# Splitting an MLP's tokens into two passes, with a seven-product scheme and DMA sums in the second

## The chip, the cores and the metric

The kernel runs on one core of one Trainium2 chip. The metric is device time in microseconds, from runs of the whole kernel; the profile beside it describes one further execution, by the hardware profiler. Five engines matter here: TensorE (PE; its weight loads are shown apart as PEld), VectorE (DVE), ScalarE (ACT), GpSimd (POOL) and SyncE (SP), which issues the DMAs. Each works through its own instructions in order; they wait for each other by semaphores.

## The reference, cut to what matters

```python
B, S, D, F, H = 1, 2048, 576, 4608, 32          # tokens, width, hidden width, heads

def reference(x, wqkv, wo, w1, w2, w3, w4):
    xn = layernorm(x)
    # A: each token attends to 8 earlier positions, 2 apart, 32 heads of 18
    q, k, v = heads(xn @ wqkv)
    a = softmax(q . k[pos - 0, 2, ..., 14] * 18 ** -0.5)      # masked where pos < 0
    A = (a . v[same positions]) @ wo
    # B: shifted mixing, then an MLP
    h  = gelu(layernorm(xn) @ w1)                # four channel quarters, shifted by +1 -1 +2 -2 tokens
    x1 = xn + shifted(h) @ w2
    B  = x1 + gelu(layernorm(x1) @ w3) @ w4      # w3: 576 x 4608, w4: 4608 x 576
    return x + A + B
```

All arrays are float32. The kernel multiplies in a reduced-precision form (`F32R`) and keeps accuracy by splitting each operand into a high and a low half: a product is high by high, high by low and low by high.

## The kernel before, in words

A multiplication on TensorE takes at most 128 rows of depth. The depth 576 is four blocks of 128 and a rest of 64; the rest's high and low halves lie together in one block of 128 rows. That gives the 14 pairs of `PAIRS`: one tile of depth 576 is 14 multiplications.

The stages, in order:

1. Projection: x is normalised, transposed and multiplied with wqkv; q, k and v go to DRAM.
2. Mixing (`mix_tile`, `mix_rem`, `w2_tile`): the shifted layer. `Y[:, t, :]`, 16 tiles of 128 tokens by 576, holds x1 afterwards. `n_turn` normalises and transposes the tiles, by way of DRAM (`put`, `get`, `split_x`), into four blocks `x1n[b]` of 512 tokens.
3. The MLP, a loop over 72 units `(c, b)` (L829): c is a block of 256 hidden channels (18), b a block of 512 tokens (4). `up(c, b, i)` (L742) makes one tile of 128 hidden channels by 512 tokens, 14 multiplications into PSUM; ACT takes the gelu twice, once rounded to the high half, once exact (L750, L751), and DVE subtracts to get the low half (L752). `down(c, b, j)` (L755) multiplies 128 tokens of the unit before with w4, 12 multiplications of 288 columns, and DVE adds the result from PSUM to `Y` in SBUF (L769). The weights of the next block are loaded by SP (`load_f`) and split by ACT and DVE (`split_w`, L167 and L168).
4. Attention itself runs on DVE during the MLP. `attention` is a generator of DVE operations, each with a price in us; `bg(us)` adds to a budget (capped at 1.5) and issues operations until it is spent. The unit calls it six times with 6.1 / 6. Eight groups of four heads; q, k and v come back from DRAM, the result goes to DRAM (`od`).
5. Output: the attention result is transposed like x1, multiplied with wo (28 multiplications of 288 columns per 128 tokens), added to `Y` on DVE and stored.

The order is written out by hand (`manual_schedule`): each engine gets its instructions in the order in which the program names them. PSUM has two tiles of 512 columns (`psa`, for up) and three of twice 512 (`psb`, for down). What a buffer of a pool holds must be read before the pool gives it out again; that, and not a plan, sets how far an engine may run ahead.

Of the kernel before, what the change touches and what calls it, by code (L numbers as in the profile page):

```python
# [19 lines left out]
HD = 18  # L20
# [25 lines left out]
def fused_block(ctx, tc, x, wqkv, wo, w1, w2, w3, w4, out):  # L46
# [7 lines left out]
    ring = ctx.enter_context(tc.tile_pool(name="ring", bufs=2, side="right", reuse_waits="tile"))  # L54
# [4 lines left out]
    Y = base.tile([128, NT, D], F32, name="Y")  # L59
# [6 lines left out]
    BN = base.tile([128, 4, 2, 6], F32, name="bn")  # L66
    ST = RT = None
# [31 lines left out]
    def transposes(src, tail, xt, col):  # L99
# [9 lines left out]
        act.copy(xt[:, 0:4, c], p0)  # L109
        for i in range(rows // 64):  # L110
            xtt, ct = tail[1][i]
            act.copy(xtt[0:64, 4, ct:ct + 128], p1[64 * i:64 * i + 64])
        dve.tensor_tensor(xt[:, 5:9, c], p0, xt[:, 0:4, c].bitcast(F32), op=ALU.subtract)  # L113
        for i in range(rows // 64):
            xtt, ct = tail[1][i]
            dve.tensor_tensor(xtt[64:128, 4, ct:ct + 128], p1[64 * i:64 * i + 64],
                              xtt[0:64, 4, ct:ct + 128].bitcast(F32), op=ALU.subtract)
# [21 lines left out]

    def get(key, xt):  # L140
        for k in ((0, 3), (3, 5)):
            sp.dma_start(xt[:, 4 + k[0]:4 + k[1], :].bitcast(F32),
                         xd[key][k[0]:k[1]].rearrange("k p c -> p k c"))

    def split_x(xt, part=None):
        raw = xt.bitcast(F32)
        if part != 1:
            act.copy(RT[64:128, :], raw[64:128, 4, :])
            act.copy(xt[0:64, 4, :], raw[0:64, 4, :])
            dve.tensor_tensor(xt[64:128, 4, :], raw[64:128, 4, :], RT[64:128, :].bitcast(F32),  # L150
                              op=ALU.subtract)
        for h in range(2) if part is None else (part,):
            hi, lo = slice(2 * h, 2 * h + 2), slice(2 * h + 5, 2 * h + 7)
            act.copy(xt[:, hi, :], raw[:, lo, :])
            dve.tensor_tensor(xt[:, lo, :], raw[:, lo, :], raw[:, hi, :], op=ALU.subtract)
# [35 lines left out]
    def z_turn(t):  # L191
        z = w1pool.tile([128, D], F32, name="z", bufs=1)
        norm(z, Y[:, t, :], 1, t)
# [14 lines left out]
    def norm_x(t):  # L208
        norm(Y[:, t, :], xtile[t], 0, t)
        if t >= 4:  # L210
            dve.tensor_copy(tail_half(t), Y[:, t, 512:])

    def ring_block(key):
        if key not in xring:
            xring[key] = ring.tile([128, 9, 512], F32R, name="xt", tag="xt")
        return xring[key]

    def prep_x(t):
        xt = ring_block(("q", t // 4))
        if t < 4:  # L220
            tail = (Y[:, t, 512:], [(xt, t * 128)])
        else:
            tail = pair_tail(ztail[t // 2], xt, t)
        transposes(Y[:, t, :], tail, xt, (t % 4) * 128)
# [33 lines left out]
    zpad = qpool.tile([16, HALO * GC], F32, name="zpad")  # L258
    pool.memset(zpad, 0.0)

    def lhs(t):
        xt = xring[("q", t // 4)]
        c = (t % 4) * 128
        return lambda s: xt[:, s, c:c + 128]
# [41 lines left out]
    def x_prep(t):  # L306
        prep_x(t)
        stats(Y[:, t, :], 1, t)

    def x_turn(t):  # L310
        stats(xtile[t], 0, t)
        norm(Y[:, t, :], xtile[t], 0, t)
        turn(Y[:, t, :], t % 4)
        stats(Y[:, t, :], 1, t)
# [30 lines left out]
    sp.dma_start(dram_ap(qkvd[8:9, 0:1, :], 0, [[(HALO + S) * GC, 16], [1, HALO * GC]]), zpad)  # L345
# [35 lines left out]
    for cg in range(1, 5):  # L381
        for t in range(4):
# [5 lines left out]
            if cg == 1:  # L388
                stats(Y[:, t, :], 1, t)
# [3 lines left out]
    def q_last(b):  # L393
        rawp.__exit__(None, None, None)
        xring["q", b] = lastp.__enter__().tile([128, 9, 512], F32R, name="xl")
# [55 lines left out]
    def load_w2(k):  # L451
        if k == 2:
            r = mupool.tile([128, D], F32, name="rz2", bufs=1)
# [13 lines left out]
    def mix_tile(b, m):  # L467
        xt = xring[("z", b)]
        ps = psa.tile([128, 512], F32, name="p1", tag="a")
        for i, (a, w) in enumerate(PAIRS):  # L470
            pe.matmul(ps, W1[:, w, m * 128:(m + 1) * 128], xt[:, a, :],  # L471
# [10 lines left out]
    def mix_rem(b):  # L482
        xt = xring[("z", b)]
        ps = psa.tile([128, 512], F32, name="p1", tag="a")
        for a in range(9):
            pe.matmul(ps, W1R[:, a if a < 5 else a - 5, :], xt[:, a, :], start=a == 0, stop=a == 8)  # L486
        u = mupool.tile([128, 512], F32, name="u", bufs=2)
        v = mupool.tile([128, 512], F32, name="v", bufs=2)
# [24 lines left out]
    def n_turn(t, zpool):  # L513
        z = zpool.tile([128, D], F32, name="rz", tag="rz")
        act.activation(z, Y[:, t, :], AF.Identity, bias=RS[2][:, t, 0:1], scale=RS[2][:, t, 1:2])
# [4 lines left out]
    def w2_tile(t):  # L520
# [10 lines left out]
        yv = Y[:, t, :].rearrange("p (h c) -> p h c", h=2)  # L531
# [423 lines left out]
```

## Time and profile before

| what | value |
|---|---|
| median of 3 runs | 1293.11 us (1292.91 to 1293.54) |
| the profiled execution's own time | 1293.05 us |
| its span, first to last instruction | 1291.3 us |
| PE busy | 1282.4 us, 99% |
| DVE busy | 939.2 us, 73% |
| ACT busy | 363.1 us, 28% |
| POOL busy | 36.7 us, 3% |
| moved by DMA | 130.45 MB, mean 101 GB/s |
| MLP stage (first up to last down) | about 313 to 1229 us |

"Busy" is the share of the span in which an engine had an instruction in hand. The rows of a profile name a line, an engine, an operation, what it writes and reads, how often it came, its busy time, the mean time of one in ns, and the idle time before it with what ended that.

### The profile page before, as it was taken

How to read it: one execution, taken by the hardware profiler on the slowest of the kernel's cores; microseconds unless marked ns; L12 is line 12 of the kernel's file. 1: busy time of each engine (PE TensorE's matmuls, PEld its weight loads, DVE VectorE, ACT ScalarE, POOL GpSimd, SP SyncE). 2: the span in 40 equal slices, each digit the busy share in tenths (PEclk: the TensorE clock that was granted, in tenths of full speed). 3: DMA queues.
4: the chain of work that ended last, by engine and by line, in shares of the span. 5: the costliest groups of instructions: out<-in, count | busy, mean ns of one | idle time of the engine just before them, and what ended most of it. 6: DMA issues, size and time to landing. Idle time of an engine off the chain costs nothing.

```text
span 1291.3 us, 18505 instructions
## 1 busy us (share of the span) xinstructions
PE 1282.4 (99%) x7642; PEld 1181.3 (91%) x7642; DVE 939.2 (73%) x1334; ACT 363.1 (28%) x593; POOL 36.7 (3%) x108
## 2 busy tenths in 40 slices
PE   8999999999999999999999999999999999999999
PEld 8999998999999998989999999999898999999998
DVE  6775424778676778888878888878888978855841
ACT  3332225444422232231222132232232231212410
POOL 2110000111000000000000000000000000000000
PEclk9999999999999999999999999999999999999999
DMA  7698994247602130221221221220222011156742
GB/s 213 180 199 172 209 195 118 69 106 195 198 29 72 31 100 20 81 82 39 82 72 49 82 73 45 85 72 30 80 94 72 30 48 46 56 121 155 211 145 83
DMA packets 165189, 130.45 MB, mean 101 GB/s; under 512 B 73569, under 2 KB 135905, under 8 KB 165105
## 3 DMA queue, kind: packets, MB, share of 16 engines
q1 hardware_dynamic: 165104, 129.27, 37.1%
q8 instruction: 60, 0.98, 0.3%
q14 instruction: 25, 0.20, 0.0%
HBM read 86.18 MB, written 42.01 MB: 99 GB/s over the span
## 4 chain that ended last, share of the span: by engine, by line
PE 97%; DVE 1%; DMA 1%; ACT 0%; issue 0%; SPq 0%; POOL 0%; ACTq 0%; DVEq 0%
PE ps L766 35%; PE p L746 35%; PE ps L182 19%; PE p L471 3%; PE ps L286 2%; PE p L486 0%; DMA raw<-in_A_wqkv_dram 0%; DVE bn L86 0%; PE p L923 0%; DVE WQ L168 0%; DMA qkvd<-stg 0%; DMA xin<-in_A_x_dram 0%; PE ps L104 0%; DVE xt L113 0%; DVE Y L96 0%
## 5 line engine op out<-in xcount | busy, mean ns | idle before, releaser
L766 PE MATMUL ps<-W,hi 128*128 128x288 f32 x2304 | 398.6, 294 | 0.0
L766 PEld LDWEIGHTS ps<-W,hi 128*128 128x128 f32 x2304 | 339.4, 188 | 6.5 <-DVE Y L769 0.2
L750 ACT ACTIVATE hi<-p 128x512 fp32r<-128x512 f32 x144 | 86.2, 599 | 582.2 <-PE p L746 582.2
L766 PE MATMUL ps<-W,lo 128*128 128x288 f32 x1152 | 245.3, 294 | 0.0
L746 PE MATMUL p<-x1n,W 128*128 128x512 f32 x1008 | 234.6, 389 | 0.0
L746 PE MATMUL p<-xt,W 128*128 128x512 f32 x1008 | 234.5, 389 | 0.0
L746 PEld LDWEIGHTS p<-xt,W 128*128 128x128 f32 x1008 | 187.3, 188 | 36.9
L746 PEld LDWEIGHTS p<-x1n,W 128*128 128x128 f32 x1008 | 187.3, 188 | 36.9
L769 DVE TENSOR_TENSOR Y<-ps,Y 128x576 f32<-128x576 f32 x288 | 211.8, 748 | 10.9 <-PE ps L766 10.7
L752 DVE TENSOR_TENSOR lo<-g,hi 128x512 fp32r<-128x512 f32 x144 | 99.4, 690 | 159.9 <-ACT g L751 159.7
L766 PEld LDWEIGHTS ps<-W,lo 128*128 128x128 f32 x1152 | 185.3, 187 | 0.0
L182 PE MATMUL ps<-WQ,xt 128*128 128x432 f32 x448 | 88.4, 359 | 0.0
L182 PEld LDWEIGHTS ps<-WQ,xt 128*128 128x128 f32 x448 | 84.3, 188 | 3.9
L698 DVE TENSOR_TENSOR prod<-q,k 128x1152 f32<-128x1152 f32 x64 | 86.3, 1349 | 0.0
L701 DVE TENSOR_REDUCE L<-prod 128x64 f32<-128x1152 f32 x64 | 86.1, 1345 | 0.0
L751 ACT ACTIVATE g<-p 128x512 f32<-128x512 f32 x144 | 85.4, 593 | 0.0
L682 DVE TENSOR_TENSOR o<-o,prod 128x1152 f32<-128x1152 f32 x56 | 75.5, 1348 | 0.0
L678 DVE TENSOR_TENSOR prod<-v,L 128x1152 f32<-128x1152 f32 x56 | 75.5, 1348 | 0.0
L167 ACT CAST W<-rawf 128x640 fp32r<-128x640 f32 x72 | 50.3, 700 | 70.3 <-PE ps L766 69.2
L168 DVE TENSOR_TENSOR W<-rawf,W 128x640 fp32r<-128x640 f32 x72 | 56.1, 782 | 0.0
L182 PE MATMUL ps<-W,h 128*128 128x288 f32 x384 | 53.4, 295 | 0.0
L471 PE MATMUL p<-xt,W 128*128 128x512 f32 x224 | 52.9, 391 | 0.3 <-ACT g L477 0.3
(117 smaller groups left out, 967.7 us busy)
## 6 DMA issues: line engine op xcount, KB each, us to landing
xd<-st SPq DMA_DIRECT2D x56, 320.0 KB, 6.0
rawf<-in_B_w_dram SPq DMA_DIRECT2D x36, 288.0 KB, 3.1
rawf<-in_B_w_dram SPq DMA_DIRECT2D x36, 256.0 KB, 3.0
xt<-xd SPq DMA_DIRECT2D x9, 768.0 KB, 6.3
qkvd<-stg SPq DMA_DIRECT2D x64, 108.0 KB, 3.8
xin<-in_A_x_dram SPq DMA_DIRECT2D x16, 288.0 KB, 3.8
xt<-xd SPq DMA_DIRECT2D x9, 512.0 KB, 7.2
q<-qkvd SPq DMA_DIRECT2D x8, 576.0 KB, 3.9
```

Of the source, the lines that this page charges most:

```text
L182: pe.matmul(ps[:, h, :n], xs(a), ws(b, h), start=i == 0, stop=i == len(PAIRS) - 1)
L471: pe.matmul(ps, W1[:, w, m * 128:(m + 1) * 128], xt[:, a, :], start=i == 0, stop=i == len(PAIRS) - 1)
L678: dve.tensor_tensor(dst, vv, Lf[:, :, w:w + 1].to_broadcast([128, TPP * GH, HD]), op=ALU.mult)
L682: dve.tensor_tensor(o, o, dst, op=ALU.add)
L698: dve.tensor_tensor(prod.rearrange("p (j h) d -> p j (h d)", h=GH), q, k[:, r0:r0 + TPP, :], op=ALU.mult)
L701: dve.tensor_reduce(Lf[:, :, w], prod, axis=AX.X, op=ALU.add)
L746: pe.matmul(ps, W3[f][:, w, :], x1n[b][:, a, :], start=n == 0, stop=n == len(PAIRS) - 1)
L750: act.activation(by_token(hi), in_order(ps), AF.Gelu_apprx_tanh)
L751: act.activation(by_token(g32), in_order(ps), AF.Gelu_apprx_tanh)
L752: dve.tensor_tensor(lo, g32, hi.bitcast(F32), op=ALU.subtract)
L766: pe.matmul(ps[:, k, :HF], h[:, col], w[:, p, k * HF:(k + 1) * HF], start=n == 0, stop=n == len(seq) - 1)
L769: dve.tensor_tensor(yv, ps[:, :, :HF], yv, op=ALU.add)
```

## The change

The MLP is done in two passes over all hidden channels: the first over the tokens 0 to 1023 (36 units, as before), the second over the tokens 1024 to 2047.

In the second pass the product of one block of 256 hidden channels with all 1024 tokens is written as two by two blocks: the weights are cut in two by channels (2 x 128) and in two by depth (2 x 288), the activations in two by depth and in two by tokens (2 x 512). Four blocks of results need eight products of blocks; sums of blocks (Winograd's form of Strassen's scheme) give them from seven. A product of depth 288 is two blocks of 128, in three high/low pairs, and a rest of 32, whose three pairs lie in one block of 96 rows: seven multiplications of 512 columns.

- `op_sums`, `op_turn`, `put_ops` make the seven activation operands once, in the first units of the first pass (ACT normalises, DVE sums and transposes, SP stores to DRAM `xo7`); `get_op` and `split_op` bring them back and split them.
- `load_w`, `w_a`, `w_s`, `w_b`, `w_c`, `w_d` load, sum and split the weights of each block; `prod` is one of the seven products; `keep` copies an intermediate result out of PSUM by ACT, `plus` adds one to a PSUM tile by DVE, `hidden` takes the gelu and its halves.
- Half of the first pass's down tiles (odd j) and all of the second's are no longer added by DVE. `spill_sum` copies them out of PSUM by ACT into a staging buffer (two in the first pass, three in the second) and POOL issues a DMA that adds them to a tile `yd[t]` in DRAM. `x` is added there too, by POOL's DMAs from DRAM to DRAM, and the sums are loaded back (`load_y`) before the output stage. The second pass's last block of down tiles is not spilled but accumulated in PSUM with the output projection.
- Attention is rationed anew (`RU`, `RD` in the first pass, from unit 7 on, `RP`, `RQ` in the second, from block 1 on); its mask is no longer a tile added by DVE but set by POOL's memsets, and its scale is applied by ACT's exponential.
- The blocks `x1n` are two tiles (high, low) instead of one, and each `get` is three loads instead of two; `Y` is two tiles, `Y1` and `Y2`; some buffers of the mixing stage are single instead of double (`u`, `v`).

```diff
-    Y = base.tile([128, NT, D], F32, name="Y")
+    Y1 = y1p.tile([128, NT // 2, D], F32, name="Y1")
+    Y2 = y2p.__enter__().tile([128, NT // 2, D], F32, name="Y2")
...
-        u = mupool.tile([128, 512], F32, name="u", bufs=2)
-        v = mupool.tile([128, 512], F32, name="v", bufs=2)
+        u = mupool.tile([128, 512], F32, name="u", bufs=1)
+        v = mupool.tile([128, 512], F32, name="v", bufs=1)
...
-        "m10": [(w2_part, 2), (pops, 1)], "m11": [(w2_part, 3), (pops, 3)],
-        "r10": [(pops, 1), (w2_part, 4)],
+        "m10": [(w2_part, 2), (pops, 1)], "m11": [(w2_part, 3), (pops, 4)],
+        "r10": [(w2_part, 4)],
...
+    def op_sums(i):
+        z = zz[i] = r2.tile([128, 8, HF], F32, name="zz", bufs=2)
+        for a, t in ((2, 8 + i), (0, 12 + i)):
+            k = dict(bias=RS[2][:, t, 0:1], scale=RS[2][:, t, 1:2])
+            act.activation(z[:, a:a + 2, 0:256], yt(t)[:, :512].rearrange("p (k c) -> p k c", k=2),
+                           AF.Identity, **k)
+            act.activation(z[:, a:a + 2, 256:], yt(t)[:, 512:].rearrange("p (k c) -> p k c", k=2),
+                           AF.Identity, **k)
+        b12, b22, b11, b21, t2, t1, t3, t4 = [z[:, k, :] for k in range(8)]
+        dve.tensor_tensor(t1, b12, b11, op=ALU.subtract)
+        dve.tensor_tensor(t2, b22, t1, op=ALU.subtract)
+        dve.tensor_tensor(t3, b12, b22, op=ALU.subtract)
+        dve.tensor_tensor(t4, b21, t2, op=ALU.subtract)
...
+    def split_op(o, p, tag):
+        t = XO[o]
+        RX = p.tile([128, 512], F32R, name="rx", tag=tag)
+        raw = t.bitcast(F32)
+        act.copy(RX[32:64, :], raw[32:64, 2, :])
+        act.copy(t[:, 0:2, :], raw[:, 3:5, :])
+        act.copy(t[0:32, 2, :], raw[0:32, 2, :])
+        act.copy(t[64:96, 2, :], raw[64:96, 2, :])
+        dve.tensor_tensor(t[32:64, 2, :], raw[32:64, 2, :], RX[32:64, :].bitcast(F32), op=ALU.subtract)
+        dve.tensor_tensor(t[:, 3:5, :], raw[:, 3:5, :], raw[:, 0:2, :], op=ALU.subtract)
...
+                    if w:
+                        pool.memset(L[0:1, 0:DIL * w, :, w:w + 1], -4.3e9)
...
+    def spill_sum(ps, t, p, bufs, tag="stg"):
+        stg = p.tile([128, D if tag == "stg" else 640 + D], F32, name="stg", tag=tag, bufs=bufs)[:, :D]
+        act.copy(stg.rearrange("p (h c) -> p h c", h=2), ps[:, :, :HF])
+        pool.dma_start(out=yd[t], in_=stg, accum_op=ALU.add)
+
+    def down(c, b, j):
+        ps = down_mm(c, b, j)
+        if j % 2:
...
+                spill_sum(ps, 4 * b + j, hp, 2)
+            return
+        yv = yt(4 * b + j).rearrange("p (h c) -> p h c", h=2)
         dve.tensor_tensor(yv, ps[:, :, :HF], yv, op=ALU.add)
...
+    def split_pair(c, p, src, n=2):
+        t = wa.tile([128, 2, 5, 128], F32R, name="wp", tag="wp", bufs=5)
+        wpair[c, p] = t
+        act.copy(t[:, 0:n, 0:3, :], src)
+        dve.tensor_tensor(t[:, 0:n, 3:5, :], src[:, :, 0:2, :], t[:, 0:n, 0:2, :].bitcast(F32), op=ALU.subtract)
+        dve.tensor_tensor(t[64:96, 0:n, 2, :], src[64:96, :, 2, :], t[64:96, 0:n, 2, :].bitcast(F32),
+                          op=ALU.subtract)
...
+    def w_s(c):
...
+        dve.tensor_tensor(s1[:, 0], a21, a22, op=ALU.add)
+        dve.tensor_tensor(a21, a21, a11, op=ALU.subtract)
+        dve.tensor_tensor(a11, s1[:, 0], a11, op=ALU.subtract)
+        dve.tensor_tensor(a12, a12, a11, op=ALU.subtract)
...
+    units = [(c, b) for c in range(NCH) for b in range(2)]
+    RU, RD = 2.1, 0.85
...
+        on = 1.0 if u >= 7 else 0.0
+        for i in range(C):
+            bg(on * RU, False)
...
+            up(c, b, i)
...
+            for j in range(4):
+                bg(on * RD, j == 1)
+                down(*prev, j)
...
+    def prod(c, k, o, ps, start, stop):
+        p, n = ((0, 0), (0, 1), (3, 0), (1, 0), (2, 0), (2, 1), (3, 1))[k]
+        w, x = wpair[c, p][:, n], XO[o]
+        seq = [(0, 0), (1, 1), (0, 3), (1, 4), (3, 0), (4, 1)]
+        for m, (a, b) in enumerate(seq):
+            pe.matmul(ps, w[:, a, :], x[:, b, :], start=start and m == 0, stop=False,
+                      skip_group_check=True)
+        pe.matmul(ps, w[0:96, 2, :], x[0:96, 2, :], start=False, stop=stop, skip_group_check=True)
...
+    for c in range(NC2):
+        RP, RQ = (0.95, 0.55) if c else (0.0, 0.0)
+        bg(RP, False)
...
+        X = psa.tile([128, 512], F32, name="p1", tag="a")
+        prod(c, 0, B11, X, True, False)
+        p1 = keep("k1", X)
+        if last:
+            hidden(*last)
+        bg(RQ)
+        dn(c, 0)
+        bg(RP, False)
+        Yp = psb.tile([128, 2, 512], F32, name="ps", tag="b")[:, 0, :]
+        prod(c, 1, B21, Yp, True, True)
+        g = plus(p1, Yp)
+        bg(RQ)
+        dn(c, 1)
+        w_a(c + 1)
+        bg(RP, False)
+        prod(c, 2, T2, X, False, False)
+        u2 = keep("k2", X)
+        hidden(c, 0, 0, None, g)
+        bg(RQ)
+        dn(c, 2)
+        w_s(c + 1)
+        bg(RP, False)
+        Z = psa.tile([128, 512], F32, name="p1", tag="a")
+        prod(c, 3, T1, Z, True, False)
+        bg(RQ)
+        dn(c, 3)
+        w_b(c + 1)
+        split_w4p(c, 0)
+        bg(RP, False)
+        prod(c, 4, T3, X, False, False)
+        u3 = keep("k1", X)
+        g = plus(u3, Z)
+        bg(RQ)
+        dn(c, 4)
+        w_c(c + 1)
+        split_w4p(c, 1)
+        load_w4(c + 1)
+        bg(RQ, False)
+        dn(c, 5)
+        hidden(c, 1, 1, None, g)
+        bg(RP)
+        prod(c, 5, T4, X, False, True)
+        hidden(c, 1, 0, X, None)
+        bg(RQ)
+        dn(c, 6)
+        w_d(c + 1)
+        load_w(c + 2)
+        bg(RP, False)
+        prod(c, 6, B22, Z, False, True)
+        g = plus(u2, Z)
+        bg(RQ)
+        dn(c, 7)
+        last = (c, 0, 1, None, g)
```

`dn(c, d)` is `down2(c - 1, d)` for c > 0: 12 multiplications for 128 tokens of the block before, and their spill.

More of the change, by code (lines that the diff above doesn't have):

```diff
@@ L646, in attention @@
     def attention(ap):
-        mask = ap.tile([128, TPP, GH, W], F32, name="mask")
-        pool.memset(mask, 0.0)
-        for w in range(1, W):
-            pool.memset(mask[0:1, 0:DIL * w, :, w:w + 1], -1e9)
         halo = HALO
@@ new lines, in add_x, with load_w @@
+    def add_x(t):
+        dve.tensor_tensor(yt(t), yt(t), xagain[t], op=ALU.add)
+    wraw, wpair, ssum = {}, {}, {}
+    wa = None
+    def load_w(c):
+        if c >= NC2:
+            return
+        r = wraw[c] = wa.tile([128, 2, 3, 256], F32, name="wr", tag="wr")
+        for k in range(2):
+            sp.dma_start(r[:, k, 0:2, :],
+                         w3[256 * k:256 * k + 256, 256 * c:256 * c + 256].rearrange("(s p) c -> p s c", p=128))
+        for k in range(2):
+            sp.dma_start(r[:, k, 2, :], dram_ap(w3, (512 + 32 * k) * F + 256 * c, [[0, 4], [F, 32], [1, 256]]))
@@ new lines, in keep, with plus, seq2 @@
+    def keep(name, ps):
+        t = h2.tile([128, 512], F32, name=name, tag=name, bufs=1)
+        act.copy(by_token(t), in_order(ps))
+        return t
+    def plus(k, ps):
+        g = h2.tile([128, 512], F32, name="g", tag="g")
+        dve.tensor_tensor(by_token(g), by_token(k), in_order(ps), op=ALU.add)
+        return g
+    def seq2(c, d):
+        b, j = divmod(d, 4)
+        col = slice(j * 128, (j + 1) * 128)
+        seq = []
+        for i in range(2):
+            hi, lo = [h[:, col] for h in hid2[c, i, b]]
+            seq += [(hi, w4t[c][:, 0, i, :]), (hi, w4t[c][:, 1, i, :]), (lo, w4t[c][:, 0, i, :])]
+        return seq
@@ new lines, in down2, with load_y @@
+    def down2(c, d):
+        ps = psb.tile([128, 2, 512], F32, name="ps", tag="b")
+        seq = seq2(c, d)
+        for n, (h, w) in enumerate(seq):
+            for k in range(2):
+                pe.matmul(ps[:, k, :HF], h, w[:, k * HF:(k + 1) * HF], start=n == 0, stop=n == len(seq) - 1)
+        spill_sum(ps, 8 + d, h2, 3)
+    yl = {}
+    def load_y(ts):
+        if ts[0] < 8:
+            tiles = [yt(t) for t in ts]
+        else:
+            y = wopool.tile([128, 4, D], F32, name="ot", bufs=2)
+            tiles = [y[:, k, :] for k in range(4)]
+        for t, y in zip(ts, tiles):
+            sp.dma_start(y, yd[t])
+            yl[t] = y
@@ L814, in o_turn, with load_wo @@
[L814 to L836 removed]
+    def load_wo(k):
+        r = worw[k] = wopool.tile([128, D], F32, name="wor", bufs=2)
+        if k < 4:
+            sp.dma_start(r, wo[k * 128:(k + 1) * 128, :])
+        else:
+            dup_tail(r, wo, 0, D)
@@ new lines, in fused_block @@
+    hidden(*last)
+    for t in range(NT):
+        b, s_ = divmod(t, 4)
+        y = yl[t] if t in yl else yt(t)
+        yv = y.rearrange("p (h c) -> p h c", h=2)
+        if t == 0:
+            load_y((12, 13, 14, 15))
+        if t in (0, 1):
+            split_x(xo[1], t)
+        if t in (4, 5):
+            split_x(xo[2], t - 4)
+        if t == 4:
+            o_get(3)
+        if t in (8, 9):
+            split_x(xo[3], t - 8)
+        seq = seq2(NC2 - 1, t - 8) if t >= 8 else []
+        col = slice(s_ * 128, (s_ + 1) * 128)
+        seq += [(xsl(xo[b], a)[:, col], Wo[w % 5][w // 5]) for a, w in PAIRS]
+        n = len(seq) - 1
```

484 lines of the change are left out of this document (285 added, 199 removed).

## The prediction

> **What bounds the kernel now.** I read the page's busy shares and its chain of work first, then the chain in order of time, then the busy time of every engine by stretch.
>
> ```profile
> span 1291.3 us, 18505 instructions
> ...
> PE 1282.4 (99%) x7642; PEld 1181.3 (91%) x7642; DVE 939.2 (73%) x1334; ACT 363.1 (28%) x593; POOL 36.7 (3%) x108
> ...
> PE 97%; DVE 1%; DMA 1%; ACT 0%; issue 0%; SPq 0%; POOL 0%; ACTq 0%; DVEq 0%
> ```
>
> TensorE is busy for 99% of the span and makes 97% of the chain that ends last. Only work taken from TensorE can shorten this kernel, and only while nothing else takes its place. The chain in order of time (start, length, what) gives the price of that work:
>
> ```profile
> 383.04 6.36 PE p L746 x28
> 389.39 6.34 PE ps L766 x48
> 395.74 6.36 PE p L746 x28
> ```
>
> 28 multiplications of 512 columns (two up tiles) take 6.36 us, 0.227 us each; 48 of 288 columns (four down tiles) take 6.34 us, 0.132 us each. The group view's mean (389 ns for the 512-column form) is the latency of one; they are pipelined, so I use the spacing. One unit, up and down of 256 hidden channels on 512 tokens, is 12.70 us. The reserve of the other engines, by stretch (PE, PEld, DVE, ACT, POOL busy, clock, DMA share, GB/s):
>
> ```profile
> 421.00:472.00 51.00, 51.00 (x307) 46.55 (x306) 41.69 (x48) 12.49 (x22) 0.00 (x0) 1.00 0.20 64
> 931.00:982.00 51.00, 51.00 (x306) 46.49 (x306) 44.86 (x53) 14.36 (x23) 0.00 (x0) 1.00 0.19 65
> 1186.00:1229.00 43.00, 43.00 (x272) 39.99 (x271) 33.69 (x54) 18.49 (x27) 0.00 (x0) 1.00 0.85 230
> ```
>
> In the middle of the MLP the DVE is 82% to 88% busy and TensorE has no gap; ACT is at a quarter. The third row shows the DMA engines 85% busy at 230 GB/s beside a TensorE that still has no gap. The granted clock is 1.00 throughout, so I expect no change from it.
>
> **The change, part by part.**
>
> *TensorE.* The first pass is 18 x 2 units, as before. In the second pass, each of 18 channel blocks made 4 x 14 = 56 up multiplications of 512 columns; it now makes seven products of seven, 49. The seventh multiplication has 96 rows instead of 128; no row here prices that, and as the 512 columns are the same I take the same 0.227 us. 18 x 7 = 126 multiplications fewer, 126 x 0.227 = 28.6 us. The down multiplications are 96 per block before and after (the last block's are folded into the output projection's accumulation), and attention, mixing and projection keep theirs. A second-pass block is 49 x 0.227 + 96 x 0.132 = 23.8 us, against 25.4 before. The profiled execution took 1293.05 us, 1.75 more than its span and 0.06 under the median of the runs, 1293.11; the sum starts there: 1293.05 - 28.6 = 1264.4 us, if all else stays covered.
>
> *DVE and ACT in the second pass.* Mean time of one:
>
> ```profile
> L769 DVE TENSOR_TENSOR Y<-ps,Y 128x576 f32<-128x576 f32 x288 | 211.8, 748 | 10.9 <-PE ps L766 10.7
> L752 DVE TENSOR_TENSOR lo<-g,hi 128x512 fp32r<-128x512 f32 x144 | 99.4, 690 | 159.9 <-ACT g L751 159.7
> L698 DVE TENSOR_TENSOR prod<-q,k 128x1152 f32<-128x1152 f32 x64 | 86.3, 1349 | 0.0
> L155 DVE TENSOR_TENSOR xt<-xt 128x1024 fp32r<-128x1024 f32 x18 | 21.4, 1222 | 2.9 <-ACT xt L154 2.6
> L750 ACT ACTIVATE hi<-p 128x512 fp32r<-128x512 f32 x144 | 86.2, 599 | 582.2 <-PE p L746 582.2
> L489 ACT COPY u<-p 128x512 f32<-128x512 f32 x4 | 2.4, 591 | 8.5 <-PE p L486 8.5
> L296 ACT COPY stg<-ps 128x864 f32<-128x864 f32 x24 | 21.1, 881 | 86.8 <-PE ps L182 70.2 <-issue 5.9 <-DMA xd<-st 4.6
> L167 ACT CAST W<-rawf 128x640 fp32r<-128x640 f32 x36 | 26.2, 727 | 0.7 <-DMA rawf<-in_B_w_dram 0.7
> L167 ACT CAST W<-rawf 128x576 fp32r<-128x576 f32 x36 | 24.2, 673 | 69.7 <-PE ps L766 69.2 <-DMA rawf<-in_B_w_dram 0.4
> ```
>
> These, too, overlap when they run back to back, as the order of time shows:
>
> ```profile
> 424.36 0.60 ACT L750 ACTIVATE hi<-p 128x512 fp32r<-128x512 f32 x1 [2.00 <-PE p L746]
> 424.85 0.59 ACT L751 ACTIVATE g<-p 128x512 f32<-128x512 f32 x1
> ...
> 425.48 0.69 DVE L752 TENSOR_TENSOR lo<-g,hi 128x512 fp32r<-128x512 f32 x1 [1.61 <-ACT g L751]
> 426.08 1.35 DVE L701 TENSOR_REDUCE L<-prod 128x64 f32<-128x1152 f32 x1
> ...
> 433.78 1.34 DVE L698 TENSOR_TENSOR prod<-q,k 128x1152 f32<-128x1152 f32 x1
> 435.05 0.75 DVE L769 TENSOR_TENSOR Y<-ps,Y 128x576 f32<-128x576 f32 x1
> 435.71 0.81 DVE L168 TENSOR_TENSOR W<-rawf,W 128x640 fp32r<-128x640 f32 x1
> 436.45 1.35 DVE L701 TENSOR_REDUCE L<-prod 128x64 f32<-128x1152 f32 x1
> ```
>
> From start to next start, DVE takes 0.60 us for 512 elements, 0.66 for 576 and 1.27 for 1152: 0.06 us and 1.05 ns per element. Per second-pass block DVE has three sums from PSUM (1.8), four low halves (2.4), three weight splits of 512 and 256 elements (0.93 each, 2.8), one of 256 and 128 (0.5), four sums of 384 (1.9) and two splits of the down weights (1.3): 10.7 us. Attention adds its rationed share, 7 x 0.95 + 8 x 0.55 = 11.05 units; an operation counted 1.3 takes 1.27, so 10.8 us. Together 21.5 of 23.8 us, 90%. By the same method the old unit is 6.1 x 0.98 + 2 x 0.60 + 4 x 0.66 + a quarter of two weight splits (0.74 + 0.66), 10.5 us or 83%, and the windows above show 82% to 88%; the method holds. A first-pass unit is 7.6 x 0.98 + 1.2 + 1.3 + 1.4 = 11.4 of 12.7, also 90%. The added work fits: zero us. If nothing overlapped, the recorded means would make it 24.1 us, 0.3 over a block; that is the other end, 0.3 x 12 = 4 us over the blocks beside attention (8 groups of 43 units; 29 units of 7.6 in the first pass leave about 123, done in block 12). ACT has 8 gelus, 3 keeps, 8 spills of 576 (between 591 and 881 ns, 0.65), four weight casts and two down-weight casts: 4.8 + 1.8 + 5.2 + 3.0 + 1.4 = 16 of 23.8 us.
>
> *The accumulating DMAs.* All 36 x 2 odd down tiles of the first pass and 17 x 8 of the second go PSUM, ACT copy, staging buffer, then a DMA issued by POOL that adds into DRAM. The old trace has no DMA from POOL and none that adds. They cost no engine on the path anything unless a staging buffer returns too late. Second pass: three buffers serve one down tile per 23.8 / 8 = 2.98 us, so each may be away for 8.9 us, 8.3 after the copy. First pass: two buffers, two tiles per unit, 12.7 us each; wide. The bounds, from landing times (KB each, us from issue to landing):
>
> ```profile
> q1 hardware_dynamic: 165104, 129.27, 37.1%
> ...
> out_dram<-Y SPq DMA_DIRECT2D x15, 288.0 KB, 2.1
> ...
> xt<-xd SPq DMA_DIRECT2D x9, 512.0 KB, 7.2
> ...
> qkvd<-stg SPq DMA_DIRECT2D x8, 432.0 KB, 7.9
> ...
> rawf<-in_A_wo_dram SPq DMA_DIRECT2D x2, 144.0 KB, 10.9
> ```
>
> The lower end is a plain store of this very tile, 2.1 us: cost zero, and nothing below it, because a tile that returns sooner frees nothing that TensorE waits for. The upper end is the slowest landing, 10.9 us: (10.9 + 0.65) / 3 = 3.85 us per tile, 0.87 more than 2.98, x 136 = 118 us. The value must lie near the store's, being the same rows of 2304 bytes; twice that, for reading as well as writing, is 4.2 us, half of what is allowed. I take zero.
>
> The Trainium skill ("DMA: Bandwidth & Descriptors", the section on the anatomy of a POOL-issued DMA) gives 2.0 us and 1 us per 436 KB for one such transfer; by it, an estimate, 2.7 us, and the sum would again gain no term. It also has a rule against this change: in "Collectives: The Full Stack" (section "The bandwidth ceiling") an adding transfer needs two source reads per chunk and so half the rate; by it the traffic of a block nearly doubles, which is the second rival's ground.
>
> POOL's queue is in order: behind a tile's DMA, waiting for its copy, stand the next tiles' DMAs and the new small memsets of attention, and behind a group's last memset stands the DVE's maximum. That is one wait of at most a tile or two per group, inside DVE's 10%.
>
> *The seam and the first stage.* In the last six units DVE gets extra work: 5.3 us of weight sums and splits and four operand splits of 0.60 + 1.14 us, 12.2 in all, against a slack of 5 x 1.3 us and 1.7 in the last four down tiles: 4 us too much, of which the three PSUM buffers hide some. I take 3 (0 to 6). Block 0 has no down tiles between its products: the product that reuses a PSUM tile directly waits for one copy (0.59), and block 1's first for four gelus at 0.49 spacing less one product of 1.6 us. Together 2 (0 to 5). The mixing stage now has single buffers where there were two, and its four DVE placements come one step earlier; 0.5 (0 to 1.5). Extra load pieces on SP, the sums of blocks (POOL and SP idle there) and the tile copies to DRAM before the passes lie under TensorE: zero; without that cover four stores of 2.1 us, 8 us at most.
>
> Sum: 1264.4 + 3 + 2 + 0.5 = 1270 us.
>
> **The rivals.**
>
> *DVE or ACT falls behind.* Both passes run DVE at 90%, and the second mixes it with waits in three directions (PSUM sums wait for TensorE, gelus for the sums, the spills stand behind those gelus on ACT). For: no stretch before had over 88%, and the wait of DVE on ACT is already 159.7 us in total above. Against: those are waits of an engine that is ahead. Half a microsecond per first-pass unit beside attention and the full 0.3 per block would be 29 x 0.3 + 12 x 0.3 = 12 us: 1282.
>
> *The adding DMAs return late; slower than before.* By the sizes in the code they move 8 x 0.295 = 2.36 MB per block, the weight loads 1.4 MB (0.79 of w3 with its repeated rests, 0.59 of w4) and attention 3.4 MB per group, 0.85 per block: 4.6 MB in 23.8 us, 193 GB/s, or 292 if the read-back counts. The third window has 230 GB/s at a share of 0.85, so at 292 the DMA engines would be the bound: 4.6 + 2.36 = 7.0 MB at 230 / 0.85 = 270 GB/s take 25.9 us per block, 2.1 over, and the landing queues up. For: that arithmetic, and POOL as an untried issuer. Against: that window's packets were small (its transposed stores move 512-byte rows), and these are 2304. Time: 1270 + 17 x 2.1 = 1306. It decides from a return of 8.3 us; at 23 us / 136 = 0.17 per tile, that is 8.8 us, the whole gain is gone.
>
> *The change doesn't do what it says.* If the 96-row multiplication or the products' loads cost TensorE more than the old rows, each block loses: at the 288-column form's overhead per column (0.132 / 288 against 0.227 / 512, 3%) it is 49 x 0.007 x 18 = 6 us, 1276. Against: weights and columns arrive as before.
>
> **How the numbers follow.** Forecast 1270 (own range 1264 to 1276), 54%. DVE or ACT behind, 1282, 18%. TensorE less quick, 1276, 6%. Late returns, 1291 to 1400, 18%, nearly all of it slower. 4% is for a chance meeting within 0.2% (2.6 us, about what a measurement of this kernel can tell from no change). Faster 0.77, same 0.04, slower 0.19. The range takes the full forecast and the DVE rival, and the near end of the late returns: 1262 to 1296.
>
> **What would show it.** Right: multiplications of the up form 126 fewer; spacing of 23.8 us per block; PE still above 97% of the span; DVE near 90% in both passes; the adding DMAs landing in 2 to 5 us. A gap of a few us at the seam. Wrong: the ACT spill waiting for a DMA, or TensorE for the spill (late returns); TensorE waiting for DVE in the middle of either pass (DVE behind); more than 0.23 us per multiplication in a product. The forecast fails if staging buffers return after 8 us, or the seam costs over 10.

## The result, and the profile after

The changed kernel takes 1391.55 us (median of 4 runs, 1387.14 to 1392.31), the kernel before, run beside it, 1293.01 (1292.89 to 1293.54): ratio 1.0754, 95% interval 1.0731 to 1.0777. It is 98.5 us slower, and 121.6 above the forecast of 1270. The profiled execution took 1387.14 us.

The page after, its span, busy shares, clock and DMA slices, DMA queues and chain by engine:

```profile
span 1385.4 us, 19880 instructions
...
PE 1295.2 (93%) x7516; PEld 1179.4 (85%) x7516; DVE 966.7 (70%) x1418; ACT 607.1 (44%) x993; POOL 236.9 (17%) x376
...
PEclk9999999999999999999999989999999999989999
DMA  7689973374967687666676837897897887989971
...
q1 hardware_dynamic: 190741, 161.52, 41.8%
q0 software_dynamic: 31680, 64.89, 31.5%
...
issue 20%; POOL 6%; PE 5%; DMA 4%; DVE 3%; ACT 2%; SPq 1%; POOLq 0%; ACTq 0%; DVEq 0%
```

TensorE has exactly the 126 multiplications fewer (7642 to 7516). Yet it is busy for 1295.2 us, more than before, and stands for 90 us where it stood for 9. The chain of work that ended last is no longer TensorE's, and its shares add up to only 41%, so it can't be used as a ledger. The new row is q0, POOL's queue: its packets take 31.5% of the time of all 16 DMA engines. Three equal stretches before, and the same three after (columns as in the prediction):

```profile
500.00:560.00 60.00, 60.00 (x362) 54.84 (x361) 50.38 (x57) 13.95 (x25) 0.00 (x0) 1.00 0.22 65
930.00:990.00 60.00, 60.00 (x355) 54.43 (x354) 50.94 (x60) 17.14 (x28) 0.00 (x0) 1.00 0.21 70
1100.00:1160.00 60.00, 60.00 (x366) 55.06 (x365) 43.35 (x51) 12.80 (x23) 0.00 (x0) 1.00 0.34 83
```

```profile
500.00:560.00 60.00, 57.94 (x345) 52.53 (x344) 52.05 (x56) 30.77 (x50) 10.80 (x14) 1.00 0.79 167
930.00:990.00 60.00, 51.13 (x276) 45.49 (x275) 43.53 (x60) 32.04 (x52) 15.16 (x22) 0.89 0.77 153
1100.00:1160.00 60.00, 52.64 (x293) 46.84 (x292) 46.27 (x62) 29.44 (x50) 14.08 (x17) 0.94 0.81 157
```

No compute engine is near its limit in the second pass (DVE 73% to 77%, ACT about half), but the DMA engines' share went from 0.2–0.3 to 0.8, and the granted clock fell below 1. What waits for what (engine, line, releaser: us in total, times, longest), over the whole span after:

```profile
DVE wp L869 <- ACT wp L868: 77.4, 16, 12.8
ACT wp L868 <- DMA wr<-in_B_w_dram: 76.6, 16, 10.0
...
ACT stg L829 <- DMA yd<-stg: 54.2, 26, 6.1
```

The largest wait for a DMA in the second pass is not for a staging buffer (38.0 of the 54.2 us fall there). It is ACT's cast of the next block's w3 (`split_pair`, called by `w_a`), 16 times, once per block. How that reaches TensorE, in order of time (start, length):

```profile
929.88 0.90 SPq L860 DMA_DIRECT2D wr<-in_B_w_dram  x2
930.83 1.24 SPq L863 DMA_DIRECT2D wr<-in_B_w_dram  x2
...
935.03 0.64 ACT L829 COPY stg<-ps 128x576 f32<-128x576 f32 x1 [2.63 <-DMA yd<-stg]
936.22 1.56 PE L996 MATMUL p<-xt,wp 128*128 128x512 f32 x6
...
942.85 0.83 ACT L868 CAST wp<-wr 128x768 fp32r<-128x768 f32 x1 [7.18 <-DMA wr<-in_B_w_dram]
943.58 0.58 ACT L1015 COPY k<-p 128x512 f32<-128x512 f32 x1
...
944.22 2.92 PE L996 MATMUL p<-xt,wp 128*128 128x512 f32 x6 [4.61 <-ACT k L1015]
```

The load is issued at 930 and used at 943, 11 us after its last piece was issued. ACT, which works in order, stands at the cast for 7.18 us. Behind it in ACT's queue is the copy `k`, which has nothing to do with the load; TensorE needs that copy before it may write the PSUM tile again, and stands for 4.61 us. The copy `k` is what TensorE waits for most: 43.0 us in 12 waits. One page row has the larger part of it, as idle time before TensorE's products:

```profile
L996 PE MATMUL p<-xt,wp 128*128 128x512 f32 x432 | 122.6, 422 | 43.8 <-ACT k L1015 32.8
```

The stall costs once more: the next six multiplications take 2.92 us instead of 1.56, because the granted clock is at half. Each of the nine stalls of 2.6 us or more from the MLP on is followed by a stretch of half clock, 3.4 us long or a multiple of it; a stall of 2.06 us (508 us) is not. The mean granted clock:

```profile
core 0: 1385.4 us, clock 0.974
```

(1 - 0.974) x 1385 = 36 us is the most that this can cost. The stretches begin 2 to 5 us after the start of a stall, mostly while TensorE still stands, and standing is counted already. They sum to 72 us, and TensorE is busy in 48 of them; half of that, an estimate of 24 us, is what the clock costs, a quarter of the loss. The Trainium skill ("TensorE: Matmul & The Clock Gate", section "Part 1: The HAM clock gate") says that the gate falls to half rate after an idle window of about 3.4 us and opens after as long a busy one. The trace agrees on the half rate and on the length of the stretches; but a stall of 2.61 us (1082 us) was already enough here.

Where the time went, against the prediction's TensorE terms alone (span 1262.7 = 1291.3 - 28.6), read from the starts of the products in the order of time; "no spills" is the run e11 below:

```
stretch                                    needed   after    no spills (e11)
start to first up tile                      313.2   313.2    312.9
first pass, to block 0's second product     458.8   481.1    468.3
block 0 to block 1                           12.7    27.8     20.4
blocks 1 to 16                              380.8   457.4    389.3
block 17 and output                          97.2   105.9     96.5
```

Of the 122.7 us too many, 76.6 lie in the sixteen blocks that run beside the spills: 28.6 us each on average instead of 23.8, from 24.1 (undisturbed) to 35.0. Another 22.3 lie in the first pass, and 15.1 in the step from block 0 to block 1, the seam.

### The profile page after: what moved, and what is told of

Read it like the earlier page. It is cut to its first block, busy times and chain, and to the rows that moved or that the text cites. A ratio compares the mean times of both kernels' runs of the same rounds, so it can differ in the third digit from the quotient of the medians.

```text
span 1385.4 us, 19880 instructions
## 1 busy us (share of the span) xinstructions
PE 1295.2 (93%) x7516; PEld 1179.4 (85%) x7516; DVE 966.7 (70%) x1418; ACT 607.1 (44%) x993; POOL 236.9 (17%) x376
## 3 DMA queue, kind: packets, MB, share of 16 engines
q0 software_dynamic: 31680, 64.89, 31.5%
## 5 line engine op out<-in xcount | busy, mean ns | idle before, releaser
L830 POOL DMA_DIRECT2D yd<-stg x208 | 182.3, 920 | 594.9 <-ACT stg L829 583.2
L823 PE MATMUL ps<-W,hi 128*128 128x288 f32 x1152 | 201.9, 297 | 14.8 <-ACT stg L829 8.5
L829 ACT COPY stg<-ps 128x576 f32<-128x576 f32 x208 | 130.8, 638 | 178.1 <-issue 71.9
L1037 PE MATMUL ps<-w4t,hi 128*128 128x288 f32 x1088 | 196.6, 304 | 8.3 <-DVE g L1020 5.3
L1037 PEld LDWEIGHTS ps<-w4t,hi 128*128 128x128 f32 x1088 | 173.6, 197 | 20.7 <-DVE g L1020 5.7
L823 PEld LDWEIGHTS ps<-W,hi 128*128 128x128 f32 x1152 | 171.7, 189 | 19.9 <-ACT stg L829 9.4
L996 PE MATMUL p<-xt,wp 128*128 128x512 f32 x432 | 122.6, 422 | 43.8 <-ACT k L1015 32.8
L823 PE MATMUL ps<-W,lo 128*128 128x288 f32 x576 | 123.7, 296 | 0.0
L1037 PE MATMUL ps<-w4t,lo 128*128 128x288 f32 x544 | 118.9, 301 | 0.0
L823 PEld LDWEIGHTS ps<-W,lo 128*128 128x128 f32 x576 | 93.3, 190 | 0.0
L869 DVE TENSOR_TENSOR wp<-wr,wp 128x512 fp32r<-128x512 f32 x54 | 37.0, 685 | 77.5 <-ACT wp L868 77.4
L868 ACT CAST wp<-wr 128x768 fp32r<-128x768 f32 x54 | 45.5, 843 | 76.6 <-DMA wr<-in_B_w_dram 76.6
```

What stands on the lines that cost most here:

```text
L823: pe.matmul(ps[:, k, :HF], h[:, col], w[:, p, k * HF:(k + 1) * HF], start=n == 0, stop=n == len(seq) - 1)
L829: act.copy(stg.rearrange("p (h c) -> p h c", h=2), ps[:, :, :HF])
L830: pool.dma_start(out=yd[t], in_=stg, accum_op=ALU.add)
L868: act.copy(t[:, 0:n, 0:3, :], src)
L996: pe.matmul(ps, w[:, a, :], x[:, b, :], start=start and m == 0, stop=False, skip_group_check=True)
L1037: pe.matmul(ps[:, k, :HF], h, w[:, k * HF:(k + 1) * HF], start=n == 0, stop=n == len(seq) - 1)
```

## The experiments

The ratios are to the kernel before, run beside each of them on the same chip.

**e1: are the broadcast loads slow because few DMA engines carry them?** The late load repeats its 32 remaining rows four times in one DMA. Here each copy is a DMA of its own.

```diff
-            sp.dma_start(r[:, k, 2, :], dram_ap(w3, (512 + 32 * k) * F + 256 * c, [[0, 4], [F, 32], [1, 256]]))
+            for a in range(4):
+                sp.dma_start(r[32 * a:32 * a + 32, k, 2, :],
+                             dram_ap(w3, (512 + 32 * k) * F + 256 * c, [[F, 32], [1, 256]]))
```

(The same for the operands' rests.)

> The loads that repeat 32 rows four (weights) or three (operands) times in one DMA are cut into one DMA per copy; nothing else changes. Theory A: such a DMA, whose outermost dimension is the 4 or 3 copies, is served by only 4 or 3 of the 16 DMA engines, stands there behind the adding packets, lands 11 us after its issue and blocks ACT. Then ACT's wait for these weights falls from 76.6 us to under 15, the 10.2 us wait of TensorE at the seam to under 3, and the time falls by 50 to 80 us, to about 1320. Theory B: the DMA engines as a whole are too busy with the adding DMAs, and every load is late. Then the wait stays over 50 us and the time within 10 us of 1391.

Measured: 1389.24 us, ratio 1.0753 (1.0706 to 1.0799). ACT's wait for the weights is 78.7 us, as before. The form of the load is not the cause; that theory fell.

**e2 and e3: what the adding, and the spills as a whole, cost.** e2 stores each tile without adding; e3 has no DMA for the spills at all. The sums are left out of both.

```diff
-        pool.dma_start(out=yd[t], in_=stg, accum_op=ALU.add)
+        pool.dma_start(out=yd[t], in_=stg)          # e2; in e3 the line is gone
```

> The spills of the down tiles store plainly over the DRAM tile instead of adding to it (the sums over the channel blocks are left out); same bytes from SBUF, same issuer, same buffers. Theory A: the packets on the few engines' way are shorter (about 120 ns for 246), so the weights' wait falls to about half, 40 us, and the time to 1330 to 1350. Theory B: with the adding gone the DMA engines have room, the wait falls under 15 us and the time under 1300.

> The spills' DMAs are left out (the copy from PSUM to the staging buffer stays; the sums of those tiles are left out). Both theories: loads land in 3 to 5 us and the waits for them go, time 1265 to 1280. If the time stays over 1300, neither DMA theory holds, and DVE or ACT is behind (the first rival of the prediction).

Measured: e2 1351.28 us (1.0449, 1.0428 to 1.047), e3 1314.09 us (1.0161, 1.0141 to 1.0182). POOL's queue in e2, then in e3:

```profile
q0 software_dynamic: 18368, 64.89, 13.9%
```

```profile
q0 software_dynamic: 1728, 3.54, 1.6%
```

With e3's row as the remainder, the 208 spills take (0.315 x 1385.4 - 0.016 x 1312.7) = 415 us of all 16 engines when they add and (0.139 x 1347.7 - 21) = 166 us when they store: 2.0 against 0.8 us for each tile of 288 KB. (By the same rows the plain store also moves a tile in 80 packets where the adding one takes 144, so not all of the difference need be the adding.) At one tile per 2.98 us, the adds alone take two thirds of the DMA engines in the second pass. The spills are worth 77 us, half of it the adding. In e2 ACT's wait for the weights falls only to 65.5 us, not to the 40 of its theory A. And e3 missed its 1265 to 1280: 44 us over the forecast remain without any spill. By its expectation neither theory of the DMAs holds then, and DVE or ACT is behind. ACT's waits in e3 show where to look:

```profile
ACT wp L867 <- DMA wr<-in_B_w_dram: 51.0, 16, 6.0
...
PE p L995 <- ACT k L1014: 12.5, 8, 6.3
```

The cast waits for its load in every block still, for about 3 us instead of 5: it is placed too early even without the spills.

**e4 and e5: is it the place of the casts in ACT's queue?** The first two casts of w3 and the sums go two down tiles later, the third cast one, with the spills (e4) and without (e5, sums left out).

```diff
         dn(c, 1)
-        w_a(c + 1)
...
         dn(c, 2)
-        w_s(c + 1)
...
         dn(c, 3)
-        w_b(c + 1)
+        w_a(c + 1)
...
         dn(c, 4)
-        w_c(c + 1)
+        w_s(c + 1)
...
         hidden(c, 1, 1, None, g)
+        w_b(c + 1)
+        w_c(c + 1)
```

> In the second pass the first use of a block's weights, a cast on ACT, moves two down tiles later (and the four sums and the later splits with it), so that a load has 16 us instead of 9.6 us before ACT's queue comes to it; the products' order, the work and the bytes are the same. Theory C: most of the loss is ACT standing at the head of its queue before a weight load that lands 11 us after its issue. Then ACT's wait for these loads falls from 76.6 us to under 20, blocks from 28.6 us on average to about 26.5, and the time from 1391 to 1340 or 1355. Theory D: DVE is saturated, and the load is only what it happens to be late with. Then blocks stay over 28 us and the time over 1380.

> The same move with the spills' DMAs left out (their sums are left out). Without the move that was 1314 us, blocks of 25.7 us on average, ACT waiting 51 us for the loads. Theory C: the wait goes, blocks near the 24.1 us that TensorE needs, time 1285 to 1295. Theory D: DVE sets the block, 25 to 26 us, and the time stays within 8 us of 1314.

Measured: e4 1356.91 us (1.0499, 1.0481 to 1.0516), e5 1300.68 us (1.0059, 1.0039 to 1.0079). The move is worth 35 us with the spills and 13 without. In e4 the wait for these weights is nearly gone, and the staging buffers are ACT's largest wait for a DMA:

```profile
ACT stg L829 <- DMA yd<-stg: 60.6, 30, 6.0
...
ACT wp L868 <- DMA wr<-in_B_w_dram: 9.4, 2, 8.4
```

In e5 13 of the 17 spacings between blocks are 24.1 us, with the full attention beside them. So DVE at 90% keeps up when the spills are away, as the prediction's sum had it, and 13 of the 44 us that e3 had left were the place of the casts.

**e6: is DVE the bound all the same?** Attention's groups 5 to 7 work on their first offset alone (7/8 of their multiplications and sums are left out, in the scores as shown and in the sum over v alike); loads and rationing stay.

```diff
                 for w in range(W):
+                    if g >= 5 and w:
+                        yield 1.3
+                        dve.tensor_copy(Lf[:, :, w], Lf[:, :, 0])
+                        yield 1.3
+                        continue
```

> In the last three of attention's eight groups DVE works out only the first of the eight offsets (the others' products and sums are left out), at the same pace of the budget and with the same loads and stores; the spills add as in the changed kernel. DVE's work in the second pass falls from about 21.5 us per block to about 12. Theory C: ACT still waits for the weight loads, time within 25 us of 1391. Theory D: blocks fall to 25 us, time under 1330.

Measured: 1357.83 us (1.0501, 1.048 to 1.0522), 34 us less, with ACT's wait for the weights unchanged at 77.5 us. That is neither theory's number (within 25 us, or under 1330). TensorE's waits for DVE's sums `g` fall from 15.8 to 5.6 us, those for `k` from 43.0 to 37.0, ACT's for staging buffers from 54.2 to 33.9. By e5, DVE isn't what keeps a block from 24.1 us without the spills; the likeliest reading is that a DVE with more reserve catches up sooner after a stall and so absorbs part of the lateness. That is only argued; beside the spills, DVE's load is a part of the loss that no run separates.

**e7: five staging buffers.** On top of e4; the room comes from one buffer each of `hi1` and `lo1`.

```diff
-        spill_sum(ps, 8 + d, h2, 3)
+        spill_sum(ps, 8 + d, h2, 5)
```

> On top of the later weight casts (1357 us): five staging buffers instead of three in the second pass, the room taken from a fourth buffer of the hidden tiles of the second token block. A tile may then be away 14.2 us instead of 8.3. If late returns of the adding DMAs are what is left in the blocks (ACT waited 60.6 us for them there), that wait falls under 10 us, the blocks from 26.6 to under 25.5 us, the time to about 1335. If the DMA engines are simply too slow for the bytes, the wait moves to other loads and the time stays within 8 us of 1357.

Measured: 1347.71 us (1.042, 1.0403 to 1.0437), 9 us less. ACT's wait for staging buffers falls from 60.6 to 17.6 us. So the late-return rival, as the prediction described it, is worth about 9 us once the casts have moved, not 21 to 130. Expected were about 1335; the miss is made largely of single long spacings (28.0, 33.2, 33.8 us), each behind a late transfer.

**e8 and e9: clearing the other queue heads.** e8 moves two operand splits from the end of the first pass into block 0, and the last group's v into another tile. e9 then moves block 0's split of the down weights behind its sixth product, puts the last group's result into the tile of q, loads wo a block earlier, and in the first pass issues two weight loads ahead of the operands' stores.

```diff
-                if j in (1, 2):
-                    split_op((T4, B22)[j - 1], hp, "g32")
...
+        if c == 0:
+            split_op(T4, h2, "g")
```

```diff
-        split_w4p(c, 0)
+        if c:
+            split_w4p(c, 0)
...
-        if c == NC2 - 2 and d in (5, 7):
+        if c == NC2 - 3 and d in (5, 7):
```

> On top of that: the last two operand splits move from the end of the first pass, where ACT stands before their loads, to just before the products that use them; and the last group's v is loaded as soon as its k is read, instead of when its first product asks for it. If the seam (16.5 us over TensorE's own time between the first two blocks) and the one long block near the end of attention (33.6 us for 24.1) are ACT's and DVE's queues standing before a late load, the seam falls by 8 to 12 us, the long block by 6 to 9, and the time by 14 to 20 below the run beside it. If they are DVE's load, neither moves by more than 3.

> On top of the run before it (1337 us), four more late transfers are taken from the heads of the queues: block 0's down weights are split after its sixth product instead of before its fifth (ACT stood 2.8 us and TensorE 6.4 us); the last attention group writes its result into the tile that held q, not into the one whose store is still under way (DVE stood 8.7 us); the first wo rows are loaded a block earlier (ACT stood 11 us); in units 2 and 3 the weight loads are issued ahead of the operands' stores (unit 4 took 20.5 us for 12.8). If late transfers at the heads of in-order queues are what is left, each of the four gives 4 to 8 us and the time is 1305 to 1315. If the cause is another (DVE's or ACT's sum of work), it stays over 1328.

Measured: e8 1337.26 us (1.0352, 1.0334 to 1.0369), e9 1334.63 us (1.0333, 1.0312 to 1.0355). In e8 the seam fell by 4.8 us instead of 8 to 12, and the long block stayed (33.2 to 32.0): v was not its cause, DVE stood for the store of the result before it. In e9 that block came to 24.1 us and the seam to 21.7, and still the median fell by 3 us, not 22 to 32 (between the two profiled executions by 10); the runs of e8 and e9 overlap. The first pass lost the 7.7 us by which its fourth unit was too long and got a stall of 7.4 us soon after, at another weight load. The last spacing but one stays at 33.1: ACT stands 8.35 us there at the cast that e4 had moved. By e9's expectation, a time over 1328 speaks for DVE's or ACT's sum of work; e11 decides that. ACT's wait for the weights of the first pass (its largest for a DMA), and the second pass as one stretch, in e9:

```profile
ACT W L182 <- DMA rawf<-in_B_w_dram: 47.1, 16, 12.3
```

```profile
793.00:1230.00 437.00, 418.04 (x2451) 375.69 (x2450) 365.27 (x513) 268.19 (x443) 118.64 (x153) 0.99 0.92 186
```

The DMA engines are nearly full, at a share of 0.92. The long waits that are left stand behind loads, at other places than before.

**e10: does adding into SBUF cost less?** On e9, the first pass's odd tiles, and x with them, are added into SBUF tiles instead of DRAM.

```diff
-        pool.dma_start(out=yd[t], in_=stg, accum_op=ALU.add)
+        pool.dma_start(out=yd[t] if t >= 8 else yt(t), in_=stg, accum_op=ALU.add)
```

> On top of that, the first pass's odd tiles of tokens 0 to 1023 and their x are added by the DMAs into the tiles in SBUF that hold them, not into DRAM; nothing is written to or loaded from DRAM for them. If the adding packets are long (246 ns mean for 2304 bytes, plain stores of that size 126 or less) because of DRAM's reading and writing, those of the first pass fall to about 150 ns, its units lose the 1.5 us spikes, and the time falls by 8 to 12 us below the run beside it. If they are long because every adding packet reads twice wherever it goes, the time stays within 4 us.

Measured: 1336.87 us (1.034, 1.0312 to 1.0368), no difference from e9. From its page, POOL's queue and its issues (KB each, median us to landing):

```profile
q0 software_dynamic: 31680, 64.89, 31.5%
...
yd<-stg POOLq DMA_DIRECT2D x136, 288.0 KB, 6.3
...
Y<-stg POOLq DMA_DIRECT2D x72, 288.0 KB, 4.2
```

POOL's queue moves the same bytes in nearly the same share of the engines' time, 31.5% against 32.8% in e9; spread over the tiles that moved, 1.8 us each instead of 2.0. Where the sum lands hardly matters. (The landing times belong to different passes and don't compare.)

**e11 and e12: e9 without spills, and with plain stores.** The edits of e3 and e2 on e9; the sums are left out.

> The e9 kernel with the DMAs of the spills left out (the copies out of PSUM stay; the sums in DRAM lack them, so the output does too). Occupancy theory: what is left of e9's loss is the DMA engines' time that the adding packets take; without them the share in the second pass falls from 0.92 to about 0.4, every load lands in time, and with the queue heads already moved the kernel comes to the sum of TensorE's work plus a few us: 1272 to 1285 us, nearly all blocks at 24.1 us. Rival, queue heads: the loads that stand at the head of ACT's and DVE's queues are late by their own order, with or without the adds; then this run keeps stalls of several us at them and stays at 1295 us or more, near e5 (1300.7). Rival, DVE: paced at 90% it can't follow; then blocks stay above 25 us.

> The e9 kernel with the spills stored plainly instead of added (same bytes written, no reading; the sums are left out, so the output lacks them). Occupancy theory: the packets of a plain store take half as long (e2: 13.9% of the engines' time for POOL's queue against 31.5%), the share in the second pass falls to about 0.7, and the time to 1295 to 1310 us, clearly below e9's 1335 and above the run without any spill. Rival, POOL's issue or the staging buffers' return: these stay as they are but for a landing of 3 instead of 6 us; with five staging buffers neither is near its limit in e9, so by this rival the time would stay within 10 us of e9.

Measured: e11 1289.36 us (0.9972, 0.9963 to 0.9982), e12 1307.54 us (1.011, 1.0095 to 1.0125). The same stretch as in e9, first e11, then e12:

```profile
793.00:1230.00 437.00, 431.78 (x2609) 393.14 (x2608) 375.85 (x531) 278.76 (x459) 2.96 (x19) 1.00 0.42 117
```

```profile
793.00:1230.00 437.00, 421.98 (x2507) 380.87 (x2505) 371.77 (x527) 277.54 (x460) 76.53 (x155) 1.00 0.61 195
```

The DMA share goes 0.42, 0.61, 0.92 from no spill over a plain store to an add; the time goes 1289, 1308, 1335. The adding costs 27 us and the storing 18, with the same number of POOL's DMAs and five staging buffers in e12 and e9. ACT's waits for staging buffers differ by 5 us between the two (16.5 and 11.4), those for the weight loads of both passes by 26 (59.4 and 33.0). That speaks for occupancy. And in e11 DVE and ACT have the work of e9, so their sum of work isn't what held e9 at 1335. e11 missed its 1272 to 1285 by 4 us. Fourteen of its seventeen spacings of blocks are 24.1 us; block 0's is 20.4, the other two are 26.2 and 25.8. What it has above TensorE's own work is in its column of the ledger:

- The seam, 7.7 us, without a late load in it. ACT's own work delays the copy `k`, and TensorE then runs at half clock:

```profile
789.38 0.83 ACT L872 CAST wp<-wr 128x768 fp32r<-128x768 f32 x1
790.12 0.58 ACT L1017 COPY k<-p 128x512 f32<-128x512 f32 x1
...
790.75 2.93 PE L998 MATMUL p<-xt,wp 128*128 128x512 f32 x6 [2.97 <-ACT k L1017]
```

- The cadence, the spacing of TensorE's multiplications when nothing stalls. 28 multiplications of 512 columns take 6.41 us (758.86 to 765.27) where they took 6.36, and a unit 12.81 us where it took 12.73 on average (both read in the order of time); a block takes 24.1 where 23.8 was forecast: 0.08 x 36 + 0.3 x 16 = 8 us. The cause was not tested.

```profile
758.86 6.57 PE L809 MATMUL p<-xt,W 128*128 128x512 f32 x28
...
765.27 0.70 PE L828 MATMUL ps<-W,hi 128*128 128x288 f32 x4
...
779.54 1.55 PE L998 MATMUL p<-xo,wp 128*128 128x512 f32 x6
780.93 0.39 PE L1000 MATMUL p<-xo,wp 96*128 96x512 f32 x1
781.16 1.55 PE L998 MATMUL ps<-xo,wp 128*128 128x512 f32 x6
```

- Single stalls in the first pass, some 6 us, and the two longer blocks, 4 us.

Of the 121.6 us over the forecast, then, 57 go with the queue heads and two more staging buffers (after to e9), 45 with the spills (e9 to e11), and 19 stay without either. Taken in the other order the spills are 77 (e3) and the queue heads 25: each makes the other dearer.

No kernel that computes everything was faster than the one before. e11 is an optimistic bound for one that keeps the sums on the chip without spilling (it has no work in place of the spills): 0.3% under the kernel before.

## Why the prediction was wrong

*Right.* The seven products: 126 multiplications fewer, and the 96-row multiplication costs no more than the others (in e11's block 0 six full ones start over 1.39 us, 779.54 to 780.93, and the 96-row one takes the next 0.23; the whole product takes 1.62 us where 1.59 was forecast). DVE at 90% of a block and ACT at 16 of 23.8 us fit, shown by e5 and e11. In e11 the TensorE part of the gain is there, less 8 us of cadence.

*Wrong, the step that failed.* "They cost no engine on the path anything unless a staging buffer returns too late", with the choice of zero between 0 and 118 us. The step asked one question of the adding DMAs, how long one tile is away, and not what they take from every other transfer. The median landing of 5.7 us stayed under the 8.3 us that the prediction allowed, and the time was lost all the same:

```profile
yd<-stg POOLq DMA_DIRECT2D x208, 288.0 KB, 5.7
```

A tile takes 2.0 us of all 16 engines, 8 of them two thirds of a block. The loads beside them land late, and a late load costs as much as a late staging buffer, because a cast that waits for it stands in front of TensorE's copies in ACT's queue. The trace of before had the warning in two rows that the prediction quoted: a DMA share of 0.2 in the MLP, and 0.85 where the output stage begins, beside landings of up to 10.9 us. It used them only for the upper bound of a return and for the rival. The price, by the last ladder (e9, e12, e11): 45 us with the queue heads cleared; 77 us with them as they are (after against e3).

*Left out of the sum.* Where a waiting instruction stands. For ACT the prediction added up the busy time (16 of 23.8 us) and let it pass; what stands behind a weight cast in ACT's queue was not looked at. Moving four pieces of it gave 35 us (e4), without a change to any engine's work. Nor did the clock get a term: "The granted clock is 1.00 throughout, so I expect no change from it" rested on a TensorE without stalls; with them about 24 us went there.

*Mis-sized.* The seam was put at 3 + 2 us, with "over 10" as failing: 15.1 after, 7.7 with its loads in time (e11). The forecast counted DVE's surplus; it was ACT's order again.

*The rivals.* Late returns (18%) was the right side, and its range of 1291 to 1400 holds the time, by its width: its own number was 1306, 85 us less. Its arithmetic of traffic, 7.0 MB per block at 270 GB/s, assumed that an added byte costs its bytes (and is half more than 4.6, where the prediction says that the traffic "nearly doubles"); the engines moved 153 GB/s at a share of 0.77 (930 to 990 us). Its place was only partly right: 54 us of ACT's waits are for staging buffers, but two more of them bring 9 us (e7). The Trainium skill's "Collectives: The Full Stack" (section "The bandwidth ceiling") states, for the reduce step of a collective, half the rate because the add needs a second read. The size agrees here: 2.5 times a plain store's engine time per tile, and about twice per packet of 2304 bytes (246 ns on average for the adding ones, 115 for SP's in the same trace). That the second read is the reason is shown by no run here. Weighing it as a rival at 18%, against the row of 2.1 us for one store, was the misjudgement; the 2.7 us that it worked out from the Trainium skill's "DMA: Bandwidth & Descriptors" met a median landing of 5.7 us under load. *DVE or ACT behind* (18%) is refuted as stated for the kernel without the spills (e5, e11); beside them its sign did come, 15.8 us of TensorE's waits for DVE's `g`, and e6 is worth 34 us. *TensorE less quick* (6 us): its sign came as well, 0.231 us per multiplication in a product (1.62 / 7) against the 0.23 that was named, and the cadence loss has its size; but the 96-row multiplication that it blamed isn't the reason.

## What to carry to other kernels

A DMA that nobody waits for is not free: cost it as a share of the 16 engines' time beside the loads already there. Here the share went from 0.2–0.3 to 0.8 in the second pass, and the weight load shown above landed about 11 us after its last piece was issued, where the old kernel's weight loads (`rawf`, 256 KB) took 3.0 in the median. For each load ask which instruction stands at the head of an in-order queue for it, and what TensorE needs from behind that: here moving the casts alone gave 35 us (e4), removing the traffic alone 77 (e3), the traffic and all the moves together 102 (e11). And stalls of TensorE can cost clock as well: here an estimate of 24 us beside 81 us of added standing.

## What was not expected of the hardware

An adding DMA of 128 rows of 2304 bytes takes 2.0 us of the 16 engines into DRAM and about 1.8 into SBUF (e10), where a plain store of the tile takes 0.8 (e2). POOL is busy for 0.92 us with issuing an adding tile (first row, the changed kernel) and 0.54 with a plain one (e2):

```profile
L830 POOL DMA_DIRECT2D yd<-stg x208 | 182.3, 920 | 594.9 <-ACT stg L829 583.2
```

```profile
L830 POOL DMA_DIRECT2D yd<-stg x208 | 113.0, 543 | 616.8 <-ACT stg L829 603.4
```

Taking work from DVE (e6) moved the time by 34 us though DVE was only 70% busy over the span, and 73% to 77% in the second pass; the reason is argued above, not shown.
